# The first two query tiles of a head pair scored in one step, with the mask written first, and the early weight conversions at another pace

## The chip, the cores and the metric

One Trainium2 chip, one of its cores. The metric is the device time of the whole program in microseconds (us), the median of several executions. Engines are called as the profile calls them: PE (TensorE matmuls), PEld (its weight loads), DVE (VectorE), ACT (ScalarE), POOL (GpSimd), SP (the queue from which transfers are issued).

## The reference

Causal attention with a decay, and then two gated layers over all tokens. B, H, S, D = 4, 8, 576, 64; the model width is 512, so there are 2304 tokens.

```python
def _attn_ref(q, k, v, f):
    scores = scale * np.matmul(q, k.transpose(0, 1, 3, 2))
    cum = np.cumsum(np.log(np.clip(f, 0.0001, 1.0)), axis=-1)
    decay = cum[:, :, :, None] - cum[:, :, None, :]
    scores = np.where(causal, -1000000000.0, scores + decay)
    scores = scores - np.max(scores, axis=-1, keepdims=True)
    attn = np.exp(scores)
    attn = attn / (np.sum(attn, axis=-1, keepdims=True) + 1e-09)
    return np.matmul(attn, v)

def _moe_ref(x, w_gate, w_val, w_out):      # 512 -> 1536 -> 512
    return (1.0 / (1.0 + np.exp(-(x @ w_gate)))) * (x @ w_val) @ w_out

def _moe2_ref(x, w_in, w_out):              # 512 -> 2048 -> 512
    h = x @ w_in
    return (h * np.clip(h + 3.0, 0.0, 6.0) / 6.0) @ w_out
```

## The kernel before

**Attention by pairs.** Two heads of one batch make a `Pair`; there are 16 pairs, four to a batch. The 576 query rows of a pair are cut into tiles s = 0 to 3 of 128 rows and a tail, s = 4, of 64 rows for each head. Each (pair, s) is one step, so there are 80 steps, in the list `units`. The first seven pairs (`UP = 7`) go through their steps upward, 0 to 4; the other nine go downward, 4 to 0.

**One step** goes through a software pipeline written out in the loop over `t`. `scores` multiplies queries and keys on PE into one PSUM bank for each head (pool `psA`, three banks, so two steps' banks overlap by one). `expo` has DVE add the decay row and take the row minimum (L334, one instruction for each head), then ACT the exponential (L342). One step later `norm` has DVE form the reciprocal of the row sums (L363, L364), and POOL multiply the rows by it (L366). Two steps later `flip` transposes the rows on PE (L384 for s = 0 and 1, L390 for s = 2 and 3, L397 and L399 for the tail) and ACT copies them into `etA` (s = 0 and 1) or `etB` (L403). Three steps later `values` multiplies by V on PE (L423), in two parts: part 0 for the columns of s = 0 and 1, part 1 for the others. `prep` transposes the next pair's queries and keys.

**The causal mask.** In the first seven pairs (`pemask`) PE adds it: after a step's scores a bf16 matmul with the identity adds the 128-column `mask` to the diagonal block (L323). In the others POOL writes a large number into the decay row in place (`hide`, L303), one step ahead. `tail_decay` (L268) does the same on POOL for the tail of the next pair.

**Weights and filler.** The weights come as 64-bit words and are converted (`convert`): three DVE instructions and one ACT instruction make a 32-bit value, then ACT or POOL writes its high part (L61, L63) and POOL in this stage the low part (L64). `conv.run(CA, EA)` adds `CA` to a due count at each step from step `C0` on, and converts one job when the count is at least 1. The first twelve of sixteen jobs are the weights of four feature tiles of the first layer; after these the pace is `CS`. When a batch's attention is stored, `Filler` places matmul groups of the first layer (twelve matmuls of 512 columns each, L437 to L439) between the steps of the next batch, 36 groups in all, spread over the steps that are left. A group is skipped until its weights are there.

**After attention** the rest of the first layer (`ff1`) and the second (`ff2`) run, with the other weights converted beside them.

The order on each engine is fixed when the program is built, by a scheduler that follows the priorities of the code with a model of the times; the lines above are its input.

Of the kernel before, what the change touches and what calls it, by code (L numbers as in the profile page):

```python
# [16 lines left out]
BIG = 1.0e30  # L17
# [3 lines left out]
def attn_moe_kernel(  # L21
# [37 lines left out]
    def split_sbuf(hi, lo, src, eng_hi, eng_lo):  # L59
# [14 lines left out]
    mask = const.tile([P, P], BF16, name="mask")  # L74
    nc.gpsimd.memset(mask, 0.0)
    nc.gpsimd.affine_select(
        out=mask, in_=mask, compare_op=ALU.is_ge, fill=BIG, base=0,
        pattern=[[-1, P]], channel_multiplier=1,
    )
# [113 lines left out]
    reads = []  # L193
# [39 lines left out]
    class Pair:  # L233


        def __init__(self, i, b, hp, order):
            self.i, self.b, self.hp, self.order = i, b, hp, order
            self.c0, self.c1 = 0, S

            self.parts = {}  # L240
            for part, ss in ((0, (0, 1)), (1, (2, 3, NQ))):
                self.parts[max(ss, key=order.index)] = part
            self.x = None
            self.up = order[0] < order[-1]
            self.pemask = self.up
# [52 lines left out]
        def hide(self, s):  # L298


            if not self.pemask:
                d = self.dc[:, :, s * P : (s + 1) * P]
                nc.gpsimd.affine_select(  # L303
                    out=d, in_=d, compare_op=ALU.is_ge, fill=BIG, base=0, pattern=[[0, 2], [-1, P]], channel_multiplier=1
                )

        def scores(self, s):

            self.sts = [psA.tile([P, 512], F32, tag="A", name="st") for j in range(2)]
            if s < NQ:  # L310
                n, qs = (s + 1) * P, slice(s * P, (s + 1) * P)
                for j, st in enumerate(self.sts):
                    r = slice(64 * j, 64 * j + 64)
                    mm = nc.tensor.matmul(  # L314
                        st[:, :n], self.qp[r, qs], self.kp[r, :n], start=True, stop=not self.pemask
                    )
                    row(mm, j == 0)
                    if j == 0:

                        after_read(mm, len(reads) + 1 - NA)  # L320
                if self.pemask:
                    for st in self.sts:
                        nc.tensor.matmul(st[:, qs], identb, mask, start=False, stop=True)  # L323
                return
            hs = S // 2
            for c, st in enumerate(self.sts):
                nc.tensor.matmul(st[:, :hs], self.qz, self.kp[:, c * hs : (c + 1) * hs], start=True, stop=True)

        def expo(self, s):

            m = sm.tile([P, 8], F32, tag="m", name="m")
# [9 lines left out]
            def ex(e, a, b):  # L341
                nc.scalar.activation(e, e, AF.Exp, bias=m[:, a : a + 1], scale=-1.0, accum_out=m[:, 2 + b : 3 + b])  # L342

            if s < NQ:
                n = (s + 1) * P
                es = [ep.tile([P, S], F32, tag="e", name="e")[:, :n] for j in range(2)]
                for j in range(2):
                    least(es[j], self.sts[j][:, :n], self.dc[:, j, :n], j)
                for j in range(2):
                    ex(es[j], j, j)  # L350
            else:
                hs = S // 2
                es = [ep.tile([P, S], F32, tag="e", name="e")]
                for c in range(2):
                    cs = slice(c * hs, (c + 1) * hs)
                    least(es[0][:, cs], self.sts[c][:, :hs], self.dt[:, cs], c, m[:, 0:1] if c else 3.0e38)
                ex(es[0], 1, 0)
# [3 lines left out]
        def norm(self, s):  # L361
            m, n = self.m[s], len(self.es[s])
            nc.vector.tensor_scalar(m[:, 4 : 4 + n], m[:, 2 : 2 + n], 1.0e-9, None, ALU.add)  # L363
            nc.vector.reciprocal(m[:, 6 : 6 + n], m[:, 4 : 4 + n])  # L364
            for j, e in enumerate(self.es[s]):
                nc.gpsimd.tensor_scalar(e, e, m[:, 6 + j : 7 + j], 1.0, ALU.mult, ALU.mult)  # L366

        def flip(self, s):

            es = self.es[s]  # L370
            if s == next(x for x in self.order if x < 2):
# [6 lines left out]
            if s < 2:  # L378
                n = (s + 1) * P
                tt = psB.tile([P, 512], F32, tag="B", name="tt")  # L380
                for j in range(2):
                    for kt in range(s + 1):
                        c = j * n + kt * P
                        nc.tensor.transpose(tt[:, c : c + P], es[j][:, kt * P : (kt + 1) * P], ident)  # L384
                jobs.append((self.etA[:, :, s * P : (2 * s + 1) * P], tt[:, : 2 * n].rearrange("p (j b) -> p j b", j=2)))
# [312 lines left out]
    def warm_up(n):  # L698
# [17 lines left out]
    CA, C0, CF, CB, CC = 0.7, 14, 0.9, (2.0, 0.5, 2.5), 1.5  # L716

    CS = 0.09
# [18 lines left out]
        Pair(i, i // NP, i % NP, list(range(NQ + 1) if i < UP else range(NQ, -1, -1)))  # L737
# [11 lines left out]
    for t in range(len(units) + 3):  # L749
# [3 lines left out]
        if t < len(units):  # L753
# [16 lines left out]
        if t < len(units) + 2:  # L770

            fill.step(20 * (done + 1) + 3 - t + (TL if done == NCA else 0))
# [18 lines left out]
        if t >= C0:  # L791
            conv.run(CA if len(conv.jobs) > 2 * NSA - 6 * NGA else CS, EA)
# [64 lines left out]
```

## Time and profile before

| | |
|---|---|
| median of three runs | 1086.24 us (1084.57 to 1086.37) |
| the profiled execution | 1084.18 us, span 1082.4 us, mean granted clock 0.993 |
| PE busy | 1055.0 us, 97% |
| DVE, ACT, POOL busy | 543.4, 349.5, 273.7 us |
| attention stage | from 8.6 us to about 326 us |
| first filler matmul | at 78 us |

The profile covers the execution from its first to its last instruction (the span). An engine's idle time stands before the instruction that ended it, with the instruction that released it. A busy PE is not PE at its peak, since the ends of matmuls are modelled: the distance from one start to the next says more.

### The profile page before, as it was taken

The page shows a single profiled execution, that of the slowest core. Times are in us where ns is not written, and L with a number is a line of the kernel's source. Part 1 is how long each engine was busy: PE and PEld are TensorE (multiplying, and loading weights), DVE is VectorE, ACT ScalarE, POOL GpSimd, SP SyncE. Part 2 cuts the span into 40 slices and gives each one's busy share as a digit, 9 for nine tenths or more (in the row PEclk, how much of TensorE's full clock was granted, in tenths as well). Part 3 has the DMA queues.
Part 4 walks back from the last instruction along what each step waited for, and adds up shares of the span by engine and source line. Part 5 has one row for each costly group of instructions (what it writes and reads, how often), then busy time and mean ns, then how long its engine had stood idle before and what let it go on. Part 6 is the DMA issues. An engine that isn't in the chain of part 4 may idle for free.

```text
span 1082.4 us, 14927 instructions
## 1 busy us (share of the span) xinstructions
PE 1055.0 (97%) x5376; PEld 831.7 (77%) x5376; DVE 543.4 (50%) x1174; ACT 349.5 (32%) x790; POOL 273.7 (25%) x368
## 2 busy tenths in 40 slices
PE   7989999999999999999999998999999999999998
PEld 4556766665767888998888886788888888888887
DVE  5788546545535861725134268873333333343343
ACT  4766457456554430303012134331111111111111
POOL 3488536435433440302102024220000000000000
PEclk9999999999999999999999999999999999999999
DMA  7977556454334421424142265710300200110010
GB/s 182 268 219 236 168 154 177 125 143 138 95 110 157 137 79 59 157 79 136 46 137 91 78 216 157 255 53 1 117 1 1 97 21 0 59 39 1 20 40 20
DMA packets 106378, 115.42 MB, mean 107 GB/s; under 512 B 62464, under 2 KB 65536, under 8 KB 106304
## 3 DMA queue, kind: packets, MB, share of 16 engines
q1 hardware_dynamic: 106208, 114.32, 34.0%
q8 instruction: 42, 0.69, 0.3%
q14 instruction: 32, 0.26, 0.1%
q10 hardware_dynamic: 96, 0.15, 0.0%
HBM read 87.63 MB, written 26.81 MB: 106 GB/s over the span
## 4 chain that ended last, share of the span: by engine, by line
PE 82%; DVE 5%; DMA 5%; issue 3%; POOL 3%; ACT 2%; SPq 0%; ACTq 0%; POOLq 0%; DVEq 0%
PE po L438 10%; PE po L439 9%; PE po L437 9%; PE ph L439 6%; PE ph L438 6%; PE ph L437 6%; PE pv L423 5%; PE st L314 4%; PE pv L438 3%; PE pv L437 3%; PE pv L439 3%; PE pg L439 3%; PE pg L438 3%; PE pg L437 3%; PE tt L390 2%
## 5 line engine op out<-in xcount | busy, mean ns | idle before, releaser
L64 DVE TENSOR_TENSOR gall<-sg,gall 128x512 fp32r<-128x512 f32 (+1 forms) x140 | 97.3, 695 | 85.1 <-ACT gall L61 55.2
L61 ACT CAST gall<-sg 128x512 fp32r<-128x512 f32 (+1 forms) x80 | 46.2, 577 | 288.2 <-DVE sg L678 288.2
L677 DVE TENSOR_SCALAR sg<-ph 128x512 f32<-128x512 f32 (+1 forms) x80 | 51.0, 637 | 158.4 <-PE ph L439 158.4
L437 PE MATMUL ph<-x,wi 128*128 128x512 f32 (+1 forms) x320 | 117.8, 368 | 0.0
L438 PE MATMUL ph<-x,wi 128*128 128x512 f32 (+1 forms) x320 | 117.7, 368 | 0.0
L439 PE MATMUL ph<-x,wi 128*128 128x512 f32 (+1 forms) x320 | 117.7, 368 | 0.0
L438 PE MATMUL po<-w,gall 128*128 128x512 f32 x288 | 112.2, 390 | 0.0
L437 PE MATMUL po<-w,gall 128*128 128x512 f32 x288 | 112.1, 390 | 0.0
L439 PE MATMUL po<-w,gall 128*128 128x512 f32 x288 | 111.4, 389 | 0.0
L366 POOL TENSOR_SCALAR e<-e,m 128x256 f32<-128x256 f32 (+4 forms) x144 | 89.4, 634 | 75.1 <-DVE m L364 38.8
L342 ACT ACTIVATE e<-e,m 128x256 f32<-128x256 f32 (+4 forms) x144 | 83.9, 585 | 55.2 <-DVE m L334 52.9
L438 PE MATMUL po<-gall,wo 128*128 128x512 f32 (+1 forms) x240 | 90.7, 379 | 2.7 <-DVE gall L64 2.7
L437 PE MATMUL pg<-x,wg 128*128 128x512 f32 (+1 forms) x240 | 90.0, 378 | 2.4 <-ACT sg L634 2.1
L437 PE MATMUL po<-gall,wo 128*128 128x512 f32 (+1 forms) x240 | 89.7, 378 | 1.9 <-POOL gall L63 1.9
L438 PE MATMUL pg<-x,wg 128*128 128x512 f32 (+1 forms) x240 | 89.8, 374 | 0.7 <-DMA x<-x_d 0.7
L439 PE MATMUL po<-gall,wo 128*128 128x512 f32 (+1 forms) x240 | 90.0, 377 | 0.0
L439 PE MATMUL pv<-x,wv 128*128 128x512 f32 (+1 forms) x240 | 89.6, 373 | 0.0
L439 PE MATMUL pg<-x,wg 128*128 128x512 f32 (+1 forms) x240 | 89.5, 373 | 0.0
L437 PE MATMUL pv<-x,wv 128*128 128x512 f32 (+1 forms) x240 | 89.5, 373 | 0.0
L438 PE MATMUL pv<-x,wv 128*128 128x512 f32 (+1 forms) x240 | 88.9, 371 | 0.0
L63 POOL TENSOR_SCALAR gall<-sg 128x512 fp32r<-128x512 f32 (+1 forms) x60 | 39.6, 661 | 190.3 <-DVE sg L636 182.7
L636 DVE TENSOR_TENSOR sg<-sg,pv 128x512 f32<-128x512 f32 (+1 forms) x48 | 29.6, 617 | 105.5 <-PE pv L439 102.4
(106 smaller groups left out, 1935.7 us busy)
## 6 DMA issues: line engine op xcount, KB each, us to landing
x<-x_d SPq DMA_DIRECT2D x88, 256.0 KB, 4.3
raw<-in_moe_w_out_dram SPq DMA_DIRECT2D x28, 512.0 KB, 3.5
dc<-cum_d SPq DMA_DIRECT2D x16, 576.0 KB, 5.2
x_d<-x SPq DMA_DIRECT2D x32, 288.0 KB, 3.0
x_d<-xs SPq DMA_DIRECT2D x32, 256.0 KB, 2.4
raw<-in_moe_w_in_dram SPq DMA_DIRECT2D x16, 512.0 KB, 4.5
raw<-in_moe_w_gate_dram SPq DMA_DIRECT2D x12, 512.0 KB, 4.3
raw<-in_moe_w_val_dram SPq DMA_DIRECT2D x12, 512.0 KB, 5.0
```

The costliest lines, as they stand in the source:

```text
L61: nc.scalar.copy(hi, src)
L63: eng_hi.tensor_scalar(hi, src, 1.0, 1.0, ALU.mult, ALU.mult)
L64: eng_lo.tensor_tensor(lo, src, hi.bitcast(F32), ALU.subtract)
L314: mm = nc.tensor.matmul(st[:, :n], self.qp[r, qs], self.kp[r, :n], start=True, stop=not self.pemask)
L342: nc.scalar.activation(e, e, AF.Exp, bias=m[:, a : a + 1], scale=-1.0, accum_out=m[:, 2 + b : 3 + b])
L366: nc.gpsimd.tensor_scalar(e, e, m[:, 6 + j : 7 + j], 1.0, ALU.mult, ALU.mult)
L423: row(nc.tensor.matmul(o[64 * j : 64 * j + 64, q0:], self.vn[:, kt, j], e, start=(kt == 0), stop=(kt == nk - 1)), kt == 0 and j == 0)
L437: nc.tensor.matmul(o, wh, xh, start=first, stop=False)
L438: nc.tensor.matmul(o, wh, xl, start=False, stop=False)
L439: nc.tensor.matmul(o, wl, xh, start=False, stop=last)
L636: nc.vector.tensor_tensor(sg, sg, pv, ALU.mult)
L677: nc.vector.tensor_scalar(sg, ph, 3.0, 0.0, ALU.add, ALU.max)
```

## The change

- Tile s = 0 has no step of its own any more. The step of s = 1 scores both: the 128 columns of s = 0 and the 256 of s = 1 lie side by side in one bank for each head. There are four steps to a pair, 64 in all.
- In the first seven pairs the mask of that step, 384 columns wide (`masks`), is written first, with `start=True`, and the scores are added onto it. In the other pairs POOL writes the masked decay of s = 0 into a tile of its own (`dz`), at the step of s = 2.
- `expo` and `norm` of that step have four sets of rows (two heads by two tiles) instead of twice two. `flip` fills two banks of 384 columns instead of one of 256 and one of 512.
- The list `banks` says which DVE instruction frees a bank, since a bank now may have two readers.
- The first conversion is due from step 8 (of four to a pair) instead of 14 (of five), at 0.3 a step up to step 16 and 0.65 after it, instead of 0.7. The later pace is 0.12 instead of 0.09. The steps of the filler's formula are 16 to a batch instead of 20.

```diff
+    masks = const.tile([P, 3 * P], BF16, name="masks")
+    nc.gpsimd.memset(masks, 0.0)
+    mask = masks[:, 2 * P :]
+    for d in (masks[:, :P], mask):
+        nc.gpsimd.affine_select(
...
-            for part, ss in ((0, (0, 1)), (1, (2, 3, NQ))):
+            for part, ss in ((0, (1,)), (1, (2, 3, NQ))):
...
-                d = self.dc[:, :, s * P : (s + 1) * P]
+                d = out = self.dc[:, :, s * P : (s + 1) * P]
+                if s == 0:
+                    out = self.dz = a1.tile([P, 2, P], F32, tag="dz", name="dz")
...
+            self.both = banks[len(banks) + 1 - NA] if len(banks) + 1 >= NA else -1
             if s < NQ:
+                tiles = [(0, 0), (1, P)] if s == 1 else [(s, 0)]
+                first = s == 1 and self.pemask
+                if first:
+                    for j, st in enumerate(self.sts):
+                        mm = nc.tensor.matmul(st[:, : 3 * P], identb, masks, start=True, stop=False)
+                        row(mm, j == 0)
+                        if j == 0:
+                            after_read(mm, self.both)
+                for c, at in tiles:
+                    n, qs = (c + 1) * P, slice(c * P, (c + 1) * P)
+                    for j, st in enumerate(self.sts):
+                        r = slice(64 * j, 64 * j + 64)
+                        mm = nc.tensor.matmul(
+                            st[:, at : at + n], self.qp[r, qs], self.kp[r, :n], start=not first,
+                            stop=at > 0 if first else not self.pemask,
+                        )
...
+            if s == 1:
+                es = []
+                for j in range(2):
+                    e = ep.tile([P, S], F32, tag="e", name="e")
+                    es += [e[:, :P], e[:, P : 3 * P]]
+                    d0 = self.dc[:, j, :P] if self.pemask else self.dz[:, j]
+                    least(es[2 * j], self.sts[j][:, :P], d0, 2 * j)
+                    least(es[2 * j + 1], self.sts[j][:, P : 3 * P], self.dc[:, j, : 2 * P], 2 * j + 1)
+                    banks.append(len(reads) - 1)
+                for a in range(4):
+                    ex(es[a], a, a)
...
+            if s == 1:
                 for j in range(2):
+                    tt = psB.tile([P, 512], F32, tag="B", name="tt")
+                    nc.tensor.transpose(tt[:, :P], es[2 * j], ident)
+                    for kt in range(2):
+                        c = (kt + 1) * P
+                        nc.tensor.transpose(tt[:, c : c + P], es[2 * j + 1][:, kt * P : (kt + 1) * P], ident)
+                    jobs.append((self.etA[:, j], tt[:, : 3 * P]))
...
-    CA, C0, CF, CB, CC = 0.7, 14, 0.9, (2.0, 0.5, 2.5), 1.5
+    CA, C0, CF, CB, CC = 0.65, 8, 0.9, (2.0, 0.5, 2.5), 1.5
-    CS = 0.09
+    CE, CS = 0.3, 0.12
...
-        Pair(i, i // NP, i % NP, list(range(NQ + 1) if i < UP else range(NQ, -1, -1)))
+        Pair(i, i // NP, i % NP, list(range(1, NQ + 1) if i < UP else range(NQ, 0, -1)))
...
-            if s > 0:
+            if s > 1:
                 p.hide(s - 1)
+            if s == 2:
+                p.hide(0)
...
-            fill.step(20 * (done + 1) + 3 - t + (TL if done == NCA else 0))
+            fill.step(16 * (done + 1) + 3 - t + (TL if done == NCA else 0))
...
-            conv.run(CA if len(conv.jobs) > 2 * NSA - 6 * NGA else CS, EA)
+            conv.run(CS if len(conv.jobs) <= 2 * NSA - 6 * NGA else CE if t < 16 else CA, EA)
```

## Rows read from the trace of the kernel before

**Rows 1.** The page: PE's busy time and share, and its granted clock in 40 slices.
```profile
PE 1055.0 (97%) x5376; PEld 831.7 (77%) x5376; DVE 543.4 (50%) x1174; ACT 349.5 (32%) x790; POOL 273.7 (25%) x368
...
PEclk9999999999999999999999999999999999999999
```
**Rows 2.** Windows from one pair's first scores to the next's: pairs 1, 3, 4, 5.
```profile
core 0: us, PE busy (x) PEld busy (x) DVE busy (x) ACT busy (x) POOL busy (x), PEclk, DMA share, GB/s
...
22.45:34.92 12.47, 11.12 (x81) 6.88 (x80) 8.55 (x39) 9.40 (x30) 7.60 (x14) 1.00 0.79 262
...
47.81:62.25 14.44, 12.09 (x88) 7.26 (x88) 13.79 (x47) 12.60 (x36) 12.70 (x15) 1.00 0.71 201
62.25:82.13 19.88, 16.83 (x103) 10.17 (x103) 14.81 (x45) 12.14 (x34) 16.55 (x21) 0.91 0.87 251
82.13:107.02 24.89, 23.69 (x146) 16.14 (x146) 21.96 (x56) 15.98 (x41) 20.05 (x25) 1.00 0.75 236
```
**Rows 3.** Timeline of PE, 5 to 100 us: six rows with idle time before them.
```profile
12.88 0.70 PE L314 MATMUL st<-kp,qp 64*128 64x256 f32 x4 [0.62 <-DVE m L334]
...
23.59 0.70 PE L314 MATMUL st<-kp,qp 64*128 64x256 f32 x4 [0.43 <-DVE m L334]
...
53.62 0.65 PE L397 MATMUL tt<-ident,e 128*128 128x128 f32 x4 [0.48 <-POOL e L366]
...
61.77 0.55 PE L390 MATMUL tt<-ident,e 128*128 128x128 f32 x3 [0.72 <-POOL e L366]
...
68.98 0.66 PE L397 MATMUL tt<-ident,e 128*128 128x128 f32 x4 [3.01 <-POOL e L366]
...
86.72 0.66 PE L397 MATMUL tt<-ident,e 128*128 128x128 f32 x4 [1.20 <-POOL e L366]
```
**Rows 4.** Timeline of POOL ahead of PE's longest wait, 63 to 70 us.
```profile
63.76 1.09 POOL L63 TENSOR_SCALAR wv<-raw 128x512 fp32r<-128x512 f32 x1
64.93 1.30 POOL L64 TENSOR_TENSOR wv<-raw,wv 128x512 fp32r<-128x512 f32 x1
66.19 1.85 POOL L268 TENSOR_SCALAR_AFFINE_SELECT dt<-dc 64x576 f32<-64x576 f32 x2
68.13 1.92 POOL L366 TENSOR_SCALAR e<-e,m 128x576 f32<-128x576 f32 x3
```
**Rows 5.** POOL's groups of instructions in pairs 3 and 4, 47.8 to 82.1 us.
```profile
L366 POOL TENSOR_SCALAR e<-e,m 128x512 f32<-128x512 f32 (+4 forms) x19 | 13.7, 735 | 1.4 <-DVE m L363 0.9 <-DVE m L364 0.4
L64 POOL TENSOR_TENSOR wg<-raw,wg 128x512 fp32r<-128x512 f32 x4 | 5.2, 1302 | 0.2
L63 POOL TENSOR_SCALAR wg<-raw 128x512 fp32r<-128x512 f32 x4 | 3.5, 882 | 2.5 <-DVE m L364 2.5
L268 POOL TENSOR_SCALAR_AFFINE_SELECT dt<-dc 64x576 f32<-64x576 f32 x4 | 3.2, 798 | 4.4 <-DVE m L334 4.3
```
**Rows 6.** Timeline of PE: a block of scores between filler matmuls.
```profile
139.58 0.40 PE L437 MATMUL po<-gall,wo 128*128 128x512 f32 x1
139.91 0.92 PE L314 MATMUL st<-kp,qp 64*128 64x384 f32 x4
140.75 0.50 PE L438 MATMUL po<-gall,wo 128*128 128x512 f32 x1
141.09 0.40 PE L439 MATMUL po<-gall,wo 128*128 128x512 f32 x1
141.32 0.40 PE L437 MATMUL po<-gall,wo 128*128 128x512 f32 x1
```
**Rows 7.** Groups of instructions by form, 0 to 470 us.
```profile
L363 DVE TENSOR_SCALAR m<-m 128x2 f32<-128x2 f32 x64 | 15.4, 240 | 26.2 <-ACT e L342 25.8
...
L366 POOL TENSOR_SCALAR e<-e,m 128x256 f32<-128x256 f32 x32 | 18.1, 578 | 12.2 <-DVE m L364 8.9 <-ACT etB L403 2.2 <-PE tt L390 1.1
...
L366 POOL TENSOR_SCALAR e<-e,m 128x128 f32<-128x128 f32 x32 | 14.4, 463 | 26.0 <-DVE m L364 15.7 <-ACT etB L403 7.1 <-ACT etA L403 2.3
...
L323 PE MATMUL st<-mask,identb 128*128 128x128 bf16 x56 | 8.1, 227 | 0.0
```
**Rows 8.** The hand-over to the first layer: one window, and PE's wait in it.
```profile
324.00:351.00 27.00, 24.40 (x113) 19.25 (x110) 14.84 (x20) 10.33 (x18) 11.20 (x11) 0.94 0.46 149
...
339.72 0.56 PE L437 MATMUL pg<-x,wg 128*128 128x512 f32 x1 [2.14 <-ACT sg L634]
```

More of the change, by code (lines that the diff above doesn't have):

```diff
@@ L73, in attn_moe_kernel @@
     nc.vector.tensor_copy(identb, ident)
[L74 to L79, printed above, removed]
+    masks = const.tile([P, 3 * P], BF16, name="masks")
[3 more added lines that the diff above has]
+        nc.gpsimd.affine_select(
+            out=d, in_=d, compare_op=ALU.is_ge, fill=BIG, base=0,
+            pattern=[[-1, P]], channel_multiplier=1,
+        )
     cum_d = dram.tile([B * H, S], F32, name="cum_d")
@@ L190, in attn_moe_kernel @@
         nc.gpsimd.memset(t[:TAIL, NQ], 0.0)
-    reads = []
+    reads, banks = [], []
     def row(mm, first):
@@ L301, in hide @@
             if not self.pemask:
[L302 removed]
+                d = out = self.dc[:, :, s * P : (s + 1) * P]
+                if s == 0:
+                    out = self.dz = a1.tile([P, 2, P], F32, tag="dz", name="dz")
                 nc.gpsimd.affine_select(
[L304 removed]
+                    out=out, in_=d, compare_op=ALU.is_ge, fill=BIG, base=0, pattern=[[0, 2], [-1, P]], channel_multiplier=1
                 )
@@ L309, in scores @@
             self.sts = [psA.tile([P, 512], F32, tag="A", name="st") for j in range(2)]
+            self.both = banks[len(banks) + 1 - NA] if len(banks) + 1 >= NA else -1
             if s < NQ:
[L311 to L321, printed above, removed]
+                tiles = [(0, 0), (1, P)] if s == 1 else [(s, 0)]
[13 more added lines that the diff above has]
+                            stop=at > 0 if first else not self.pemask,
+                        )
+                        row(mm, j == 0 and at == 0 and not first)
+                        if j == 0 and at == 0 and not first:
+                            after_read(mm, self.both)
+                if self.pemask and not first:
                     for st in self.sts:
@@ L348, in expo @@
                     least(es[j], self.sts[j][:, :n], self.dc[:, j, :n], j)
+                    banks.append(len(reads) - 1)
                 for j in range(2):
@@ L356, in expo @@
                     least(es[0][:, cs], self.sts[c][:, :hs], self.dt[:, cs], c, m[:, 0:1] if c else 3.0e38)
+                    banks.append(len(reads) - 1)
                 ex(es[0], 1, 0)
@@ L362, in norm @@
             m, n = self.m[s], len(self.es[s])
-            nc.vector.tensor_scalar(m[:, 4 : 4 + n], m[:, 2 : 2 + n], 1.0e-9, None, ALU.add)
-            nc.vector.reciprocal(m[:, 6 : 6 + n], m[:, 4 : 4 + n])
+            nc.vector.tensor_scalar(m[:, 8 : 8 + n], m[:, 4 : 4 + n], 1.0e-9, None, ALU.add)
+            nc.vector.reciprocal(m[:, 12 : 12 + n], m[:, 8 : 8 + n])
             for j, e in enumerate(self.es[s]):
-                nc.gpsimd.tensor_scalar(e, e, m[:, 6 + j : 7 + j], 1.0, ALU.mult, ALU.mult)
+                nc.gpsimd.tensor_scalar(e, e, m[:, 12 + j : 13 + j], 1.0, ALU.mult, ALU.mult)
         def flip(self, s):
             es = self.es[s]
-            if s == next(x for x in self.order if x < 2):
+            if s == 1:
                 self.etA = et.tile([P, 2, 384], F32, tag="etA", name="etA")
@@ L377, in flip @@
             jobs = []
-            if s < 2:
-                n = (s + 1) * P
-                tt = psB.tile([P, 512], F32, tag="B", name="tt")
+            if s == 1:
                 for j in range(2):
[L382 to L385, printed above, removed]
+                    tt = psB.tile([P, 512], F32, tag="B", name="tt")
[4 more added lines that the diff above has]
+                    jobs.append((self.etA[:, j], tt[:, : 3 * P]))
             elif s < NQ:
```

6 lines of the change are left out of this document (3 added, 3 removed).

## Prediction

> **What bounds the kernel now.** I read the page first: PE is busy 97% of the span [rows 1]. So a change to attention pays only if it takes idle or slow time away from PE; work that it saves on DVE, ACT or POOL is worth nothing by itself. The windows come next, cut at the start of each pair's scores. Pair 1 takes 12.47 us with PE busy for 11.12; there is no filler and no conversion in it. Pair 3 does the same work in 14.44 us and pair 4, which has a little filler, in 19.88. POOL explains the difference: it is busy for 7.60 us in pair 1, but for 12.70 in pair 3 and 16.55 in pair 4, nearly all of the window [rows 2]. From pair 6 on PE has filler, and rows of PE with idle time become rare; so the place to look at is the first 107 us. Third I listed PE's waits there. Two short ones, 0.62 and 0.43 us, stand before the scores of s = 1, on the DVE reading of s = 0: three banks serve two heads, and the second step's first bank pair is not free before. Four others, 0.48, 0.72, 3.01 and 1.20 us, stand before transposes that wait for POOL's normalising [rows 3]. Last, POOL's own order ahead of the longest one: two conversion instructions, then the decay of the next tail, and only then the rows that PE waits for [rows 4]. Right behind it the granted clock of pair 4 is 0.91, which says that a part of it ran at the lower level, 1.2 instead of 2.4 GHz [rows 2].
>
> **Conversions.** A job costs POOL 1.302 + 0.882 = 2.18 us; normalising and tails cost it (13.7 + 3.2) / 2 = 8.4 us in each of pairs 3 and 4 [rows 5], where conversions slow them, and 7.6 in pair 1 [rows 2]. By the due count, before, jobs fall on steps 15, 16, 18, 19 (pair 3) and 21, 22, 24 (pair 4): POOL needs 8.4 + 4 x 2.18 = 17.1 and 8.4 + 3 x 2.18 = 14.9 us, where PE without filler needs 11 to 12.5. So POOL is the bound, and its excess is PE's wait. After, jobs fall on steps 11 (pair 2), 14 (pair 3), 16 and 18 (pair 4), 20 and 21 (pair 5): 10.6 us in pair 3 and 12.8 in pair 4. The first is under PE's need, the second about at it. What there is to win: the four waits on POOL, 0.48 + 0.72 + 3.01 + 1.20 = 5.41 us [rows 3], and the slow clock of pair 4: a mean of 0.91 between levels of 1 and 0.5 is 18% of 19.88 us at half speed, of which half is lost, (1 - 0.91) x 19.88 = 1.79 us [rows 2]; 7.2 in all. The bounds are 0 (the queue orders jobs just as badly) and 7.2. I take two thirds, 4.8, since pair 4 stays near the bound. The filler's start moves from pair 4.8 to pair 5.0 by the same formulas (step 24 of five to a pair, 20 of four), as all 36 groups have to run anyway and 34 fall inside attention both before and after by the due counts; I cost it at nothing. What hides that is that PE has attention work then; without this cover, 0.2 x 12.5 = 2.5 us. The waiting for weights costs nothing while the twelfth job is there at step 30 and the group that needs it, the ninth, is due at step 31. The four slow jobs fall on pairs 7 to 14 before and 9 to 16 after, under filler. SP issues the same transfers; a conversion's loads come earlier by a pair at most.
>
> **The merged scores.** The two waits of s = 1 on s = 0 go, since there is no such hand-over any more: 1.05 us [rows 3], bounds 0 (the wait comes back before s = 2) and 1.05. A block of scores among filler costs PE more than its columns: starts of filler are 0.23 us apart, but 0.33 ahead of the block and 0.34 behind it, so 0.21 for going in and out [rows 6]. One block of every pair goes: 16 x 0.21 = 3.4 us at most, nothing at least, as in the first pairs the neighbours are transposes. The mask adds: four matmuls of 128 bf16 columns become two of 384, so 2 x 384 - 4 x 128 = 256 columns more, at 2.4 GHz 0.11 us, in seven pairs 0.75. The rows have no mask wider than 128 [rows 7]; an upper end is three times its 227 ns for each, 7 x (2 x 3 - 4) x 0.227 = 3.2. I take 0.75, since the row's 227 ns is mostly latency at PE's end. So blocks and mask together: between -3.4 and +3.2, I take -1.5. DVE saves a sum and a reciprocal for a pair, 16 x 0.24 us for the first alone [rows 7]; it is off the path: nothing. The transposes are the same six in number, the copies have 768 columns before and after: nothing.
>
> **The longer chain.** All four exponentials must be done before the one sum of row totals, and POOL then has 2 x 0.463 + 2 x 0.578 = 2.08 us in one piece ahead of the transposes of that step; for s = 1 alone it had 1.16 [rows 7]. The excess is 0.92 us. Behind it on POOL wait the next rows' normalising and, in the last nine pairs, `hide`, now two in a row at the step of s = 2. Two steps of lag are half a pair instead of two fifths, 0.1 x 12.5 = 1.2 us more, which covers it on average. Bounds: nothing, and 0.92 in each of five pairs without filler, 4.6. I take 1.0.
>
> A rule of the Trainium skill speaks against the merging. The page "PSUM — Partial Sum Buffer", section Terms, has it that TensorE writing and another engine reading one bank in the same quadrant at once is an error. By this rule DVE may not begin with s = 0 until PE has written s = 1 into the same bank. Four scores of that width take 0.70 us [rows 3], so by the rule the sum is up to 5 x 0.7 = 3.5 us worse in the pairs without filler, 1083.4 instead of 1079.9; without it, nothing changes. No row of before shows which, as each bank has one block there.
>
> **The sum**: -4.8 - 1.05 - 1.5 + 1.0 = -6.35, so 1084.18 - 6.35 = 1077.8 us for an execution like the profiled one (1082.4 span and 1.8 around it). The median shown is 2.06 above that execution, so for a median I say 1086.24 - 6.35 = 1079.9. What attention saves passes to the end, since PE is the bound behind it. One spot there is free to move: at the hand-over PE waits 2.14 us and the clock is 0.94 of 27 us, another 1.6 [rows 8]. It may vanish or double, 3.7 either way, as it hangs on which job ACT has in front. I leave it out of the sum and take it into the range.
>
> **Rivals.**
> *The chain takes back what POOL gives* (slower). The merged step's rows come too late for their transposes in every pair. For: 2.08 us in one piece on POOL, an in-order queue, and a first DVE reading that may begin only when the s = 1 half of its bank is written too, up to 0.70 us later [rows 3]. Against: from pair 6 on PE has filler to put between, and waits on POOL are absent from its timeline. It decides from (4.8 + 1.05 + 1.5) / 16 = 0.46 us a pair on; at the full 0.92 for 16 pairs, 14.7 us, the time is 1086.24 - 7.35 + 14.7 = 1093.6; at two thirds of it, 1088.7. Chance 0.13.
> *The pace does not matter* (near no change). POOL's bunching stays because pair 4 is still without filler, and the slow clock with it: -1.05 - 1.5 + 1.0 = -1.55, so 1084.7. For: 12.8 us of POOL in pair 4. Against: one job instead of four in pair 3. Chance 0.24, of which two thirds within the bound of no change.
> *All of it goes*: -7.2 - 1.05 - 3.4 + 0.75 = -10.9, so 1075.3. For: the waits have one cause. Against: pair 4. Chance 0.13.
>
> **How the numbers follow.** About 0.2%, 2.2 us, is what a measurement of this kernel can tell from no change. The forecast has 0.50 with an own range of 1077 to 1083.5. Faster: 0.50 + 0.13 + 0.08 of the second rival = 0.71. Same: 0.16. Slower: 0.13. The range reaches from 1074.5, the last rival and a little of the hand-over, to 1087, which leaves out most of the slower rival.
>
> **What would show it.** In the profile after: POOL's busy share in pairs 3 and 4 falls below 0.85; no wait of PE over 1.5 us and a clock of 1.00 before 100 us; pair 4 without its filler near 13 us; no wait of PE on DVE before the merged scores; from pair 6 on each pair shorter by 0.1 to 0.2 us at equal filler. I am wrong if PE's waits on POOL move to the transposes of the merged step, if the first DVE reading starts late and PE waits for it, or if the hand-over at the end of attention grows.

## The result: 1069.3 us, beyond the forecast's range

The changed kernel takes 1069.27 us (median of four runs, 1068.96 to 1069.79), the kernel before 1086.30 beside it: a ratio of 0.9838 [0.9811, 0.9864], so 17.0 us or 1.6% faster. The forecast was 1079.9 in a range of 1074.5 to 1087.0. The direction was right; the size was too small, and the range did not hold it.

The profiled execution takes 1068.96 us, span 1066.8, which is 15.2 us less than that of before. All of it lies inside attention: its last instruction on PE starts at 311.0 us instead of 326.2, and what follows, to PE's last start, takes 751.8 us before and 751.5 after.

From the page of the kernel after, each engine's busy time, share and count of instructions. PE is as full as before:

```profile
PE 1045.2 (98%) x5362; PEld 830.5 (78%) x5362; DVE 532.9 (50%) x1142; ACT 348.5 (33%) x790; POOL 272.4 (26%) x369
```

Windows of the kernel after, from one pair's first scores to the next's, for pairs 1, 3, 4 and 5, and the hand-over:

```profile
core 0: us, PE busy (x) PEld busy (x) DVE busy (x) ACT busy (x) POOL busy (x), PEclk, DMA share, GB/s
20.41:32.04 11.63, 11.63 (x84) 7.08 (x83) 7.68 (x34) 8.29 (x27) 7.44 (x14) 1.00 0.89 248
45.26:59.19 13.93, 12.41 (x89) 7.84 (x88) 11.29 (x41) 10.99 (x32) 9.33 (x13) 1.00 0.85 241
59.19:71.89 12.70, 12.29 (x90) 7.61 (x89) 11.21 (x37) 11.02 (x33) 10.86 (x15) 1.00 0.77 229
71.89:88.58 16.69, 16.69 (x93) 11.07 (x92) 12.49 (x40) 12.15 (x35) 13.95 (x19) 1.00 0.85 234
324.00:351.00 27.00, 25.73 (x107) 21.16 (x108) 23.91 (x32) 11.99 (x20) 12.57 (x11) 0.94 0.41 128
```

Pair 3 now has 9.33 us of POOL in its window and pair 4 has 10.86, where it was 12.70 and 16.55 [rows 2]. The clock of pair 4 is 1.00 where it was 0.91. The timeline of PE after, every row from 5 to 100 us that has idle time before it:

```profile
10.07 0.63 PE L286 MATMUL tq<-ident,qn 128*128 128x128 f32 x4 [0.48 <-DMA qn<-in_q_dram]
12.95 0.92 PE L333 MATMUL st<-kp,qp 64*128 64x384 f32 x4 [0.52 <-DVE m L354]
51.85 1.13 PE L333 MATMUL st<-kp,qp 64*128 64x512 f32 x4 [1.52 <-DVE m L354]
64.22 0.66 PE L430 MATMUL tt<-ident,e 128*128 128x128 f32 x4 [0.41 <-POOL e L399]
```

Of the waits on POOL in [rows 3], 5.41 us in all, one of 0.41 is left. The two waits of s = 1 on s = 0 are gone too, but one of the same kind now stands before s = 3 of pair 3, 1.52 us, and one before s = 2 of the first pair. [rows 3] are not all the rows with idle time that before has up to 100 us: six others come to 2.70, two of them before later scores, 0.95 and 0.19, and two on POOL, 0.33 and 0.56. From the timeline of PE before, the longest of the six:

```profile
51.12 0.92 PE L314 MATMUL st<-kp,qp 64*128 64x384 f32 x4 [0.95 <-DVE m L334]
```

So waits on DVE before scores come to 2.0 us where they came to 2.2. From 9 us to the end of attention PE is idle (the length of the stretch less PE's busy time in it) for 12.2 us before and 7.2 after. Before also has one stretch of 3.4 us at half the granted clock, worth 1.7 us, and after has none there. Together that is 6.7 us. The rest, 8.5 us, comes from places where no idle time is shown, and the experiments had to find it.

### The profile page after: what moved, and what is told of

Read it like the earlier page. It is cut to its first block, busy times and chain, and to the rows that moved or that the text cites. A ratio compares the mean times of both kernels' runs of the same rounds, so it can differ in the third digit from the quotient of the medians.

```text
span 1066.8 us, 14817 instructions
## 1 busy us (share of the span) xinstructions
PE 1045.2 (98%) x5362; PEld 830.5 (78%) x5362; DVE 532.9 (50%) x1142; ACT 348.5 (33%) x790; POOL 272.4 (26%) x369
## 4 chain that ended last, share of the span: by engine, by line
PE 84%; DMA 5%; DVE 4%; issue 3%; POOL 2%; ACT 2%; SPq 0%; ACTq 0%; POOLq 0%; DVEq 0%
PE po L472 10%; PE po L471 10%; PE po L470 10%; PE ph L472 6%; PE ph L470 6%; PE ph L471 6%; PE pg L470 4%; PE pg L471 4%; PE pg L472 4%; PE pv L470 4%; PE pv L471 4%; PE pv L472 4%; PE pv L456 3%; PE st L333 3%; PE tt L423 2%
```

## The experiments

Before ran beside every kernel. Medians in us; a ratio is to before on the same chip, with its 95% interval. The other columns are of the one profiled execution. "Attention" is the start of attention's last PE instruction; what lies behind it, to PE's last start, takes 750.7 to 754.6 us in all of these kernels, whatever was edited ahead of it. "Idle" is PE's idle time from 9 us to there. "Slow clock" is what stretches at half the granted clock cost in it, 1.7 us for each 3.4. "Cut" counts the blocks of scores or values in which the matmuls of one head ran apart from the other's, as e9 explains below.

| kernel | median (before) | ratio | attention | idle | slow clock | cut |
|---|---|---|---|---|---|---|
| before | 1086.30 | 1 | 326.2 | 12.2 | 1.7 | 12 |
| after | 1069.27 (1086.30) | 0.9838 [0.9811, 0.9864] | 311.0 | 7.2 | 0 | 6 |
| e1 pace alone | 1082.31 (1086.93) | 0.9957 [0.9940, 0.9973] | 322.4 | 15.1 | 0 | 7 |
| e2 merging alone | 1072.82 (1086.93) | 0.9868 [0.9842, 0.9894] | 315.3 | 11.2 | 1.7 | 5 |
| e3 after, merged in pairs 0 to 6 only | 1079.19 (1086.93) | 0.9925 [0.9901, 0.9949] | 320.9 | 8.7 | 0 | 15 |
| e4 after, merged in pairs 7 to 15 only | 1071.00 (1086.93) | 0.9852 [0.9827, 0.9876] | 310.2 | 10.5 | 0 | 1 |
| e5 before, filler groups whole | 1084.35 (1086.53) | 0.9980 [0.9965, 0.9994] | 326.0 | 17.5 | 3.4 | 7 |
| e6 after, filler groups whole | 1075.60 (1086.53) | 0.9897 [0.9876, 0.9918] | 319.4 | 11.6 | 3.4 | 7 |
| e7 after, merged step's mask last | 1070.00 (1086.53) | 0.9843 [0.9823, 0.9863] | 311.0 | 8.0 | 0 | 5 |
| e8 as e4, filler groups whole | 1082.77 (1086.53) | 0.9966 [0.9950, 0.9982] | 322.8 | 17.5 | 5.1 | 2 |
| e9 before, heads kept side by side | 1076.46 (1086.69) | 0.9907 [0.9877, 0.9938] | 318.4 | 14.0 | 3.4 | 0 |
| e10 after, heads kept side by side | 1064.95 (1086.69) | 0.9804 [0.9787, 0.9821] | 307.2 | 9.9 | 0 | 0 |
| e11 as e9, with e1's pace | 1077.49 (1086.69) | 0.9915 [0.9892, 0.9939] | 321.1 | 14.1 | 6.8 | 0 |
| e12 before, filler at four of five steps | 1079.85 (1086.69) | 0.9940 [0.9921, 0.9959] | 322.0 | 11.6 | 1.7 | 9 |
| e13 as e10, filler offered five times a pair | 1069.29 (1085.69) | 0.9839 [0.9818, 0.9859] | 309.6 | 10.4 | 1.7 | 0 |
| e14 as e9, filler at four of five steps | 1073.02 (1085.69) | 0.9874 [0.9851, 0.9898] | 313.6 | 11.9 | 0 | 0 |
| e15 as e10, merged block parted by a dummy | 1070.32 (1085.69) | 0.9857 [0.9831, 0.9884] | 309.4 | 9.0 | 0 | 0 |

**The two halves of the change, apart (e1 to e4).** e1 is before with the new pace, scaled to five steps a pair; e2 is after with the old one, scaled to four; e3 and e4 are after with the steps of some pairs as before. The three edits, in this order:

```diff
-    CA, C0, CF, CB, CC = 0.7, 14, 0.9, (2.0, 0.5, 2.5), 1.5
-    CS = 0.09
+    CA, C0, CF, CB, CC = 0.52, 10, 0.9, (2.0, 0.5, 2.5), 1.5
+    CE, CS = 0.24, 0.096
...
-    CA, C0, CF, CB, CC = 0.65, 8, 0.9, (2.0, 0.5, 2.5), 1.5
-    CE, CS = 0.3, 0.12
+    CA, C0, CF, CB, CC = 0.875, 11, 0.9, (2.0, 0.5, 2.5), 1.5
+    CE, CS = 0.875, 0.1125
...
-        Pair(i, i // NP, i % NP, list(range(1, NQ + 1) if i < UP else range(NQ, 0, -1)))
+        Pair(i, i // NP, i % NP, list(range(LO(i), NQ + 1) if i < UP else range(NQ, LO(i) - 1, -1)))
```

`LO(i)` is 1 for a merged pair and 0 for one that keeps five steps. In e3 and e4 the pace and the filler's formula are kept pair by pair, so that the nine downward pairs have five offers of filler in e3 and four in e4.

> The kernel before with the new conversion pace alone, turned into steps of five to a pair (from step 10 at 0.24 a step, from step 20 at 0.52, later 0.096). In the order as built, PE's work up to the end of attention falls into 353 stretches of one kind (scores, masks, transposes, values, filler), against 387 before and 311 after. Stretch theory: each border between kinds costs PE about 0.2 us, so 34 borders fewer than before give 1086.3 - 6.8 = 1079.5. POOL theory: the pace alone takes away the waits on POOL and the slow clock of pair 4, 4.8 to 7.2 us, so 1079 to 1081.5, with PE's waits gone between 53 and 90 us and nothing changed later. The two tell apart by where: stretch theory wants part of the gain after 110 us.

> The changed kernel with the old conversion pace in pairs (from step 11 at 0.875 a step, later 0.1125). 314 stretches on PE in the order as built, nearly those of the changed kernel. Stretch theory: 1069.3 + 3 x 0.2 = 1070. POOL theory: the waits on POOL and the slow clock near 70 us come back, 5 to 7 us, so 1074 to 1076.

> The changed kernel with the first two tiles as one step in the seven upward pairs alone, five steps to a pair in the nine downward ones; same pace by pair. 357 stretches on PE. Stretch theory: 1069.3 + 46 x 0.2 = 1078.5. If the gain sits in the first pairs (masks, hand-over waits, POOL): under 1072.

> The changed kernel with the first two tiles as one step in the nine downward pairs alone; same pace by pair. 304 stretches on PE, fewer than the changed kernel's 311. Stretch theory: 1069.3 - 7 x 0.2 = 1067.9, at most 1069.3. If merging itself pays in each pair (two hand-over waits, less masking): seven pairs without it lose about 1 us each, 1074 to 1077.

The pace alone gives 4.6 us, the merging alone 14.1. On top of e1, merging gives 3.1 in the seven upward pairs (e3) and 11.3 in the nine downward ones (e4). By the end of attention it is 1.5 and 12.2. So the surprise is the merging. But e1 to e4 also differ in their idle time and in their cuts (e3 has 15, e4 one), so these differences are not yet the price of a merged step.

Nor is e1's 4.6 what the waits and the clock gave over the whole stage. The timeline of PE in e1, three of its waits:

```profile
52.26 0.66 PE L390 MATMUL tt<-ident,e 128*128 128x128 f32 x4 [1.12 <-POOL e L366]
66.68 0.66 PE L397 MATMUL tt<-ident,e 128*128 128x128 f32 x4 [1.32 <-POOL e L366]
...
321.82 0.87 PE L423 MATMUL pv<-etA,vn 128*64 128x256 f32 x8 [2.60 <-ACT etA L403]
```

The first two are the only waits on POOL that are left between 45 and 100 us, 2.44 for 5.41, and no stretch of slow clock is left in attention. Up to the first scores of pair 6 PE spends 21.8 us beyond the columns of its matmuls at 2.4 GHz, 6.0 less than in before. At the end of attention only 3.8 of that is left: behind 110 us the rows with idle time come to 8.6 us instead of 2.8. Idle time and slow clock together are 15.1 us, for 13.9 before. So the 3.8 are about the size of what e1's five fewer cuts are worth, 4.2 us by the prices below.

**Is every change of the kind of work on PE dear? (e5, e6, e8)** My first theory was that each change costs some 0.15 to 0.2 us: PE's built order goes from one kind of block to another 387 times before and 311 times after, and e1 to e4 roughly followed that count. These three raise the priority of the rest of a begun filler group, so that nothing is put between its matmuls:

```diff
-        nc.tensor.matmul(o, wh, xh, start=first, stop=False)
-        nc.tensor.matmul(o, wh, xl, start=False, stop=False)
-        nc.tensor.matmul(o, wl, xh, start=False, stop=last)
+        with tc.high_priority() if whole and not first else ExitStack():
+            nc.tensor.matmul(o, wh, xh, start=first, stop=False)
+        with tc.high_priority() if whole else ExitStack():
+            nc.tensor.matmul(o, wh, xl, start=False, stop=False)
+            nc.tensor.matmul(o, wl, xh, start=False, stop=last)
```

> The kernel before, with nothing merged and the old pace; only the scheduler's priority is raised for the second to last matmul of each filler group, so that the twelve stay together. 315 stretches on PE up to the end of attention, against 387. Stretch theory: the time beside the columns that is not idle was 0.147 us a stretch in all six traces so far, so 72 fewer give 10.6 us: 1076. Rival, that what the merged step itself removes (a block of scores, a hand-over to DVE, a round of normalising) makes the gain: 1086, no change, or slower, since attention's rows now wait up to 2.7 us for a filler group to end.

> The changed kernel with filler groups kept together in the same way. 285 stretches against 311. Stretch theory: 26 x 0.147 = 3.8 us less, 1065.5. Rival: the merged step leaves too little slack for a group of 2.7 us, PE idles more, 1069 to 1072.

> Merged in the nine downward pairs alone, with filler groups kept together. 286 stretches, against 304 without the latter, which had 1071.0. Stretch theory: 18 x 0.147 = 2.6 us less, 1068.4, above the run with everything merged and kept together by no more than its idle time in the first pairs. Rival (no slack): 1071 or more.

The theory fell as it stood. e5 has 315 such changes, 72 fewer than before, and gained 2.2 us; e6 has 285, 26 fewer than after, and lost 6.3; e8 has 286 and lost 11.8 against e4. Holding filler together makes other work late. e6's attention ends 8.4 later than after's, with 4.4 more of idle time, 3.4 more of slow clock and one more cut block; e8's ends 12.6 later than e4's, with 7.0 and 5.1 more. e5 proves less by itself, since it also has five fewer cuts and 7.0 us more of idle time and slow clock. The rows show the price of a border directly. The timeline of PE before, transposes between filler:

```profile
319.61 0.39 PE L437 MATMUL po<-gall,wo 128*128 128x512 f32 x1
319.84 0.60 PE L390 MATMUL tt<-ident,e 128*128 128x128 f32 x4
320.19 0.48 PE L438 MATMUL po<-gall,wo 128*128 128x512 f32 x1
320.50 0.39 PE L439 MATMUL po<-gall,wo 128*128 128x512 f32 x1
```

The four transposes and the filler matmul behind them take 320.50 - 319.84 = 0.66 us, which is what they take by themselves: four transposes 0.11 apart and 0.23 for the filler. PE's waits by releaser, 9 to 326 us, first after and then e6 (us in total, times, longest):

```profile
PE st L333 <- DVE m L354: 2.0, 2, 1.5
...
PE pv L456 <- DVE qz L300: 0.3, 1, 0.3
```
```profile
PE st L333 <- DVE m L354: 4.0, 3, 1.5
PE pv L456 <- DVE qz L300: 3.2, 5, 0.9
```

**The place of the mask (e7).** The merged step's masks go behind its scores, 128 columns a tile, as before:

```diff
-                if first:
-                    for j, st in enumerate(self.sts):
-                        mm = nc.tensor.matmul(st[:, : 3 * P], identb, masks, start=True, stop=False)
...
-                if self.pemask and not first:
-                    for st in self.sts:
-                        nc.tensor.matmul(st[:, qs], identb, mask, start=False, stop=True)
+                    if self.pemask:
+                        for st in self.sts:
+                            nc.tensor.matmul(st[:, at + c * P : at + n], identb, mask, start=False, stop=True)
```

> The changed kernel with the merged step's mask behind the scores as before: scores of the first tile, its two masks, scores of the second, its two masks. 328 stretches against 311. Stretch theory: 17 x 0.147 = 2.5 us more, 1071.8. Rival, that the early mask fills a wait that PE has anyway: the same plus what idle time comes back in the first pairs, 1073 to 1075. If the mask's place does not matter: 1069.

It makes 0.7 us of difference, inside the interval, and attention ends at 311.0 in both: no effect of the mask's place and width can be measured.

**Two heads out of step (e9 to e11).** After that I stopped listing idle time and read the distances from one start to the next, block by block. The timeline of PE before, in a downward pair, and further up one block of s = 0:

```profile
107.02 0.49 PE L314 MATMUL st<-kp,qp 64*128 64x128 f32 x4
107.44 0.28 PE L323 MATMUL st<-mask,identb 128*128 128x128 bf16 x2
...
195.12 0.75 PE L423 MATMUL pv<-etB,vn 128*64 128x320 f32 x2
195.81 0.50 PE L439 MATMUL pg<-x,wg 128*128 128x512 f32 x1
196.24 1.12 PE L314 MATMUL st<-kp,qp 64*128 64x512 f32 x2
197.29 2.27 PE L423 MATMUL pv<-etB,vn 128*64 128x320 f32 x18
199.49 0.44 PE L384 MATMUL tt<-ident,e 128*128 128x128 f32 x2
199.86 1.12 PE L314 MATMUL st<-kp,qp 64*128 64x512 f32 x2
```

None of these rows shows idle time, and yet much of it is lost. A block of values has twenty matmuls, ten for each head, each on its own half of the array's columns. Here two of one head went ahead alone, taking 195.81 - 195.12 = 0.69 us, and the other eighteen then took 199.49 - 197.29 = 2.20. The same block in one piece takes 2.20 to 2.21, as in e9 and in after, below. So the two went for nothing: 0.69 us lost. This pattern, x2 and then x18, stands seven times in the trace of before (158.88 to 308.47) and not once in after. It is the same with the scores of s = 3: the two heads use separate halves of the array's rows, and x2 at 196.24 takes 1.05 us, as does x2 at 199.86, where x4 takes 1.06 in e9. The cut costs the whole block again.

The Trainium skill, page "TensorEngine Tiling (Array Packing)", section Key Properties, says that separate tiles of the array work in parallel; the trace agrees, since one head alone takes as long as two.

e9 is before and e10 after, with no such cuts: the first matmul of values also waits for the other head's copy, and the rest of a begun block of scores or values has a raised priority. e11 adds e1's pace to e9.

```diff
+                    with tc.high_priority() if PRIO and j else ExitStack():
                       mm = nc.tensor.matmul(
                         st[:, :n], self.qp[r, qs], self.kp[r, :n], start=True, stop=not self.pemask
...
+                    if one and WAIT:
+                        tc.add_manual_dep(
+                            mm.ins, self.copied[part].ins.name,
```

> The kernel before, nothing merged, old pace. Two additions: the first matmul of a part of the values waits until ACT has copied the rows of both heads, and the other matmuls of a block of scores or values have a raised priority, so that nothing comes between the two heads. In the order as built no block is cut (64 blocks of scores, 32 of values; before 67 and 44). Theory of cut heads: two heads run on PE at the same time only side by side; a cut costs 0.4 us in a block of values and up to 1 us in one of scores, 5.7 us in all before, and each piece more costs its going in and out, 0.2 us: 1079 to 1081. Rival (the gain is the merged step's own, or latency): 1086, or slower by the added wait.

> The changed kernel with the same two additions. No block is cut (48 and 32 blocks; 52 and 37 without them). Theory of cut heads: its own cuts cost 1.7 + 1.0 us, so 1066 to 1067. Rival (latency): the added wait costs what it brings, 1069 or more.

> The kernel before with the same two additions and with the new conversion pace (as in the run of the pace alone, 1082.3). Theory of cut heads: cuts cost that run 2.6 us and their borders as much, so 1077 to 1078.5. What is left between this run and the changed kernel with the additions is the merged step's own: one block of scores (0.2 to 0.4 us) and one hand-over for each of 16 pairs, 8 to 12 us.

The timeline of PE in e9, the same pair:

```profile
192.32 0.40 PE L450 MATMUL pg<-x,wg 128*128 128x512 f32 x1
192.65 1.13 PE L316 MATMUL st<-kp,qp 64*128 64x512 f32 x4
193.71 2.28 PE L429 MATMUL pv<-etB,vn 128*64 128x320 f32 x20
195.91 0.44 PE L386 MATMUL tt<-ident,e 128*128 128x128 f32 x2
```

Without cuts before gains 10.2 us (e9) and after 4.3 (e10). In PE's built order before has 24 pieces that leave the heads unequal (two to a cut block: nine blocks of values, three of scores), after has 12, e9 and e10 none. What a cut costs goes with the columns that one head computes alone. In the trace of before seven blocks of values lose 0.69 each and two narrow ones 0.57, two blocks of scores of 512 columns 1.05 and one of 128 columns 0.42: 8.5 us. In after it is 0.84 for two blocks of scores of 384 columns, 0.52 for one of 256, and 0.68, 0.57 and 0.47 for three of values: 3.9. That is near what was measured, with something for the borders of the added pieces; attention ends 7.8 and 3.8 earlier, although e9 has 3.5 and e10 2.7 more of idle time and slow clock. Half of the cuts were lost by the change, and nothing in it aims at them: the scheduler's order came out otherwise. e11 is no faster than e9 by the medians. Its attention ends 2.7 later, but its trace, that of the slowest of its four executions, has 3.4 us more of slow clock: where no cuts are left, the new pace on before brings nothing that I can measure.

**How often filler is offered (e12 to e14).** With four steps to a pair the filler is placed at four points instead of five.

```diff
-        if t < len(units) + 2:
-            fill.step(20 * (done + 1) + 3 - t + (TL if done == NCA else 0))
+        if t < len(units) + 2 and (t >= len(units) or units[t][1] > 0):
+            left = sum(s > 0 for _, s in units[t : 20 * (done + 1)]) + 3
+            fill.step(left + (TL if done == NCA else 0))
```

e14 is e9 with the same edit; e13 is e10 with a second call of `fill.step` at each step of s = 1.

> The kernel before with filler placed at four of a pair's five steps (not at that of the first tile), the due count as before over fewer steps. It changes how often filler is offered, as the merged kernel does, and nothing else: 43 blocks of values and 65 of scores, nearly as before. Theory of cut heads: 1085 to 1086. Rival, that fewer places for filler make the gain: 1078 to 1081.

> The changed kernel without cuts (e10, 1064.95) with filler offered five times a pair, twice at the merged step, as before the change. If the number of places is what the merge saved: 1069 to 1072. If it is the block or the waits: 1064 to 1066.

> The kernel before without cuts (e9, 1076.46) with filler offered at four of the five steps. If the number of places counts by itself: 1070 to 1072, most of the way to e10. If what e12 gained came through the cuts that it happened to lose (six blocks of scores down to two) and through waits: 1075 to 1078.

Four offers on before gain 6.8 us (e12), and attention ends 4.2 earlier. Most of that is cuts again: three blocks of values at 0.69 and two of scores at 1.05 fewer, two narrow ones of values at 0.57 more, 3.0 us, and 0.7 is idle time. Without any cuts four offers gain 3.4 (e14; attention ends 4.8 earlier), and a fifth offer in e10 loses 4.3 (attention 2.4 later, and what lies behind it takes 753.7 instead of 751.4). The traces say where: e9 has 3.4 us of slow clock and 2.1 of idle time more than e14, e13 1.7 and 0.5 more than e10. From the windows of e9 and then of e14, the same stretch of time in each:

```profile
core 0: us, PE busy (x) PEld busy (x) DVE busy (x) ACT busy (x) POOL busy (x), PEclk, DMA share, GB/s
235.00:255.00 20.00, 17.08 (x106) 10.56 (x106) 11.13 (x45) 12.75 (x36) 8.82 (x15) 0.91 0.54 166
235.00:255.00 20.00, 19.35 (x133) 11.62 (x133) 12.99 (x49) 14.74 (x42) 10.72 (x20) 1.00 0.50 156
```

So waits and slow clock cover both differences in attention (5.5 for 4.8, 2.2 for 2.4), and a price of an offer by itself is not shown. e14's interval overlaps e9's, and e13's touches e10's.

**What one block costs by itself (e15).** The timeline of PE after: a merged block among other work, and a block of values in one piece.

```profile
153.39 0.60 PE L290 MATMUL tk<-ident,kn 128*128 128x128 f32 x4
153.92 0.93 PE L333 MATMUL st<-kp,qp 64*128 64x128 f32 x8
154.77 0.50 PE L470 MATMUL pg<-x,wg 128*128 128x512 f32 x1
155.11 0.40 PE L471 MATMUL pg<-x,wg 128*128 128x512 f32 x1
...
191.87 2.28 PE L456 MATMUL pv<-etB,vn 128*64 128x320 f32 x20
194.08 0.66 PE L286 MATMUL tq<-ident,qn 128*128 128x128 f32 x4
```

The row is labelled by its first matmul; it holds 128 and 256 columns for both heads. It takes 154.77 - 153.92 = 0.85 us. A block of 128 columns takes 0.42 (107.02 to 107.44, above), one of 384 takes 0.84 [rows 6], one of 512 takes 1.06 (e9, above). That is 0.21 us for every 128 columns and 0.21 more for the block, however wide. So the block that disappears should save 0.21 inside and, among filler, the 0.21 at its borders [rows 6]. e15 tests this: it writes sixteen columns that nobody reads, with the whole array, between the two halves of the merged block, in the nine downward pairs.

```diff
                 for c, at in tiles:
+                    if at and not first:
+                        with tc.high_priority():
+                            row(nc.tensor.matmul(self.sts[1][:, 3 * P : 3 * P + 16], identb, masks[:, :16], start=True, stop=True), False)
```

> e10 with a matmul over all 128 rows, 16 columns wide, between the two halves of the merged block in the nine downward pairs; it writes columns that nobody reads, and 16 columns take 7 ns. If a block's own going in and out is the cost: 0.2 to 0.4 us a pair, 1.8 to 3.6 us in all, 1067 to 1068.5, and the merged block with its neighbour grows from 0.86 us to 1.05 to 1.25 in the trace. If only the number of steps counts: 1065, block 0.87 to 0.95.

The timeline of PE in e15:

```profile
150.15 0.49 PE L338 MATMUL st<-kp,qp 64*128 64x128 f32 x4
150.58 0.18 PE L333 MATMUL st<-masks,identb 128*128 128x16 bf16 x1
150.69 0.70 PE L338 MATMUL st<-kp,qp 64*128 64x256 f32 x4
151.32 0.50 PE L485 MATMUL pg<-x,wg 128*128 128x512 f32 x1
```

151.32 - 150.15 = 1.17 us instead of 0.85: 0.11 for the dummy and 0.21 for a second entry into the 64-row block. Nine times 0.32 is 2.9 us; attention ends 2.2 later than in e10, with 1.0 less of idle time, so 3.1 later beside it. The median is 5.4 us above e10's, but 3.2 us of that lie behind attention in the profiled executions (754.6 against 751.4), where the dummy is not.

The same Trainium skill page and section says that changing the tiling mode, not just the tile, drains TensorE. The traces agree: a block that uses half of the rows pays the fixed 0.21 us once, and pays it again as soon as one matmul of the whole array stands in between, while the fallen theory had also counted borders between filler and transposes, which are both `128*128` and have no such price in the rows above. That the drain is the whole of the 0.21 no run here shows.

## Why the prediction was wrong

**Conversions: the signs came true, the size partly by luck.** POOL's busy share in pair 3 is 0.67, in pair 4 0.855 (I had said below 0.85 in both), the clock is 1.00, and pair 4 without filler takes 12.70 us ("near 13"). One wait is 1.52 us where I allowed 1.5. But the term of -4.8 was to be found in waits and slow clock, and e1, which measures -4.6, has no less of them over the whole of attention: 4.6 us that went before 110 us came back behind it as other waits, 5.8 us, and the number came out because there were fewer cuts. On the merged kernel the pace does what I said: from e2 to after, idle time and slow clock go from 12.9 to 7.2. The hand-over's -1.05 came near its lower bound: waits on DVE before scores fell by 0.15, since they came back before later scores, and the list that I summed left out the waits of 0.95 and 0.19 of that kind. Waits and clock as a whole, -4.8 - 1.05 + 1.0 = -4.85 in my sum, came to -6.7.

**What PE does while it shows no idle time: the step that failed.** My working looked for lost time only in PE's idle rows, in its clock and at a block's two borders. It gave -1.5 to blocks and mask and nothing to the rest. On top of the pace the merging brought 13.0 us (after against e1). In the profiled executions the 15.2 us are 6.7 of waits and clock, 4.6 of cuts, and so 3.9 are left for blocks and mask, of which the sum had 1.5. What was missing:

- *Cuts between the heads*, put at nothing. They were in the trace of before, 8.5 us of them, and I never read them: I had stopped at 107 us because PE shows few idle rows behind it. PE's ends are modelled, so a head that works alone looks as busy as two. After has 3.9 us of them.
- *The block's own entry.* I wrote that a block costs 0.21 us for going in and out, "16 x 0.21 = 3.4 us at most, nothing at least, as in the first pairs the neighbours are transposes". The rows in hand gave more: 0.21 at the borders and another 0.21 in front of the columns, 0.42 for a block. Transposes as neighbours are some discount, but not the whole: in the trace of before the last transpose ahead of a block of scores starts 0.20 us before it (median of 40), where transposes are 0.11 apart, so 0.09 in front; behind a block it is 0.02 with masks and nothing to 0.15 with transposes. That makes about 0.3 to 0.42 a block, 5 to 6.7 for 16. The runs give the lower end: from e14 to e10, both free of cuts and slow clock and with four offers, attention ends 6.3 us earlier, 2.0 of it idle time, and the other 4.3, with the mask's 0.6 added, are 0.31 a pair.

In a chain of medians: before 1086.7, without cuts 1076.5 (e9), with four offers 1073.0 (e14), merged and repaced 1065.0 (e10), with after's own cuts 1069.3. The steps depend on each other, and each brings its own waits and stretches of slow clock, so the split has an uncertainty of a few us.

**From pair 6 on: too little.** I expected 0.1 to 0.2 us a pair at equal filler. Taking each pair's window less the columns of its matmuls at 2.4 GHz, two heads side by side counted once, pairs 6 to 15 lost 4.1 us each before and 3.6 after: about 0.6 less. This sum holds idle time and slow clock as well. For the whole of attention it is 69.2 before and 54.1 after, and 9.3 of the difference lie in the first six pairs, where I looked, 5.8 behind them.

**The mask: right to be small.** From the timeline of PE, a wide pair of masks after, and a narrow pair before:

```profile
30.97 0.49 PE L325 MATMUL st<-masks,identb 128*128 128x384 bf16 x2
31.30 0.27 PE L414 MATMUL tt<-ident,e 128*128 128x128 f32 x1
...
39.97 0.28 PE L323 MATMUL st<-mask,identb 128*128 128x128 bf16 x2
40.09 0.39 PE L384 MATMUL tt<-ident,e 128*128 128x128 f32 x2
```

Two masks of 384 columns take 0.33 us, for 0.24 of four narrow ones, 0.6 us in seven pairs, for the 0.75 that I took; e7 says that the old place would be no better.

**The longer chain: it did not come.** I took +1.0. The 0.41 us before 100 us is the only wait on POOL there, and over the whole of attention such waits come to 1.4 us, for 6.3 before. The rule on banks that I weighed (the Trainium skill, "PSUM — Partial Sum Buffer", section Terms) fits the trace: DVE's first reading starts at 154.88, 0.96 us after the block's start and 0.11 after its end, though the columns of s = 0 come first; so it is in eight of the nine downward pairs (0.95 or 0.96). From the timeline of DVE after:

```profile
154.88 0.29 DVE L354 CUSTOM_DVE_ANT_0 e<-st,dz 128x128 f32<-128x128 f32 x1 [0.20 <-PE st L333]
```

DVE waits there for PE's semaphore, as the program has it, so the trace agrees with the rule and does not test it. It may be part of the two waits of 0.52 and 1.52 us before later scores, 2.0 in place of the 2.2 that such waits took before; in the downward pairs no wait on that reading shows, so the 3.5 us of the rule's sum did not arise.

**The rivals.** "The pace does not matter" fell with e1 as a number; that e11 is no faster than e9 speaks for it on before without cuts, and from e2 to after attention ends 4.3 us earlier, though the intervals of their medians overlap. "The chain takes back" fell with the windows; "all of it goes", 1075.3, came nearest and was still 6 us too high, because it too gave the blocks 3.4 at most and the cuts nothing. The hand-over behind attention neither vanished nor doubled: PE waits 2.87 us instead of 2.14, at the same clock of 0.94.

The runs also give a faster kernel than either: e10, 1064.95 us, 0.9804 [0.9787, 0.9821] of before.

## What to carry to other kernels

When PE is busy 97%, its idle rows show only a part of its lost time: read the distance from one start to the next against the columns, and look above all for blocks on half of the array (64 rows or 64 columns) that come as x2 and x18 instead of x20. Keep the two partners of such a block side by side, by a dependency on the later of their inputs, and count for each block its entry and its borders beside its columns, so that one wide block beats two narrow ones. Any edit can reorder a scheduled kernel, so before crediting the edit, compare three things in both traces: how the blocks are cut, PE's idle time over the whole stage, and the stretches of slow clock. A total that agrees with the forecast, like e1's, proves little until its parts do.

## What the runs showed of the hardware that I had not expected

- A block of fp32 scores on 64 rows takes 0.42, 0.84 and 1.06 us for 128, 384 and 512 columns: 0.21 for every 128 and 0.21 once for the block, beside 0.10 and 0.11 at its borders. One matmul of 16 columns on the whole array in its midst costs 0.32.
- One head's scores alone take 1.05 us, those of both heads together 1.06.
- Changes between filler and transposes, both on the whole array, show no price in the rows: four transposes and a filler matmul take 0.66 us.
- The granted clock fell to half for 3.4 us (once for 6.8) in nine of the seventeen traces within attention, each time just behind waits of PE, 3.01 us in before, 1.65 and 2.76 in e9. Each 3.4 us costs 1.7, as much as two cuts, and the kernels differ in it by up to 6.8 us.
